# Attention scores by 128 queries of one head, the two heads in the row halves of TensorE's array, for ten of 24 head pairs of a fused attention and gated MLP kernel

## The chip, the cores and the metric

The kernel runs on one core of one Trainium2 chip. The metric is the time of one execution on the device in microseconds (us).

## The reference

Causal attention over 4 batches of 12 heads, 448 positions, head size 64, in single precision; its output, with the heads joined to 768 features, goes through a gated MLP with a spatial product:

```python
scores = scale * np.matmul(q, k.transpose(0, 1, 3, 2))
scores = np.where(np.triu(np.ones((seq, seq), dtype=bool), k=1), -1000000000.0, scores)
attn = np.exp(scores - np.max(scores, axis=-1, keepdims=True))
attn = attn / (np.sum(attn, axis=-1, keepdims=True) + 1e-09)
x = np.matmul(attn, v)                       # heads joined: 4 x 448 x 768
h = np.maximum(x @ w_in, 0.0)                # 1024 features
u, v = h[..., :512], h[..., 512:]
v_n = (v - mean(v)) / np.sqrt(var(v) + 1e-06)
v_s = np.einsum('ts,bsd->btd', w_spatial, v_n) + b_spatial[None, :, None]
out = (u * v_s) @ w_out
```

## The kernel before

The kernel handles the 48 heads as 24 pairs, six a batch (`attend`, one call a pair). A pair's steps: load q and k (`load`), turn them so that the head size lies on the partitions, multiply to scores, add the causal mask and find each row's extreme (VectorE, L757), exponential with its row sum (ScalarE, L769), reciprocal of the sum (L782, L790), scale the weights, turn them, multiply with V (L893), and copy the result into `xT` as a high and a low half-precision part (L911, L916). When a batch's six pairs are there, `ffn` does its matmuls (L1118, 50 us or so of TensorE a batch); chains of them can begin with the pairs that are ready, and otherwise serve as filling between the steps of later pairs.

There are three kinds of pair, set by `TURNED` and `SINGLE`:

- Pairs 0 to 8: q and k are turned by TensorE (`qk_turn`, L578) and kept in single precision. q is laid out in blocks of 128 columns, 64 queries of head 0 in the upper rows and of head 1 in the lower, zeros elsewhere (`q32`, cleared once in `constants`); so one product of the full array (L736) gives the scores of 64 queries of both heads. Seven such products a pair, against 64, 128, ... 448 keys, lie in four PSUM banks (`BANKS`). The weights, in single precision, are scaled by GpSimd, ScalarE or VectorE (`even`, L427, L425, L423), turned by TensorE in 16 blocks (L807) and copied to `et` (L827, L829); the product with V is in single precision, one head in each column half of the array.
- Pairs 9 to 14: the same scores, with widths rounded up to 128 columns, but the weights are split into two half-precision parts (L425, L857) and turned by three DMA transposes (L870); the product with V takes three half-precision terms.
- Pairs 15 to 23: q and k too are split into half-precision parts (two squares and a sum for a scale, L495 and L504; scaling and splitting at L427 and L459), turned by a DMA transpose (L639) and copied across partitions by two local DMAs (L647). The scores are two half-precision products for each 64 queries and head (L746, L747), one head in each column half.

PSUM has four slots `ps` for scores and transposes, one `px` and three `pf` for the feed-forward chains. The order of all work is written out before the run by a planner (`Plan`): it gives each operation a cost in ns for each engine that can do it, spreads the free ones over ScalarE, VectorE and GpSimd, and simulates the engines, taking by rank, which comes from due times. The constants `TUNE`, `SLACK`, `EARLY` and others set the due times and slacks. Each engine and the DMA queue of SyncE then run their instructions in that order.

Of the kernel before, what the change touches and what calls it, by code (L numbers as in the profile page):

```python
# [7 lines left out]
F32 = mybir.dt.float32  # L8
# [240 lines left out]
def kernel(  # L249
# [11 lines left out]
    nc = tc.nc  # L261
# [254 lines left out]
    def constants():  # L516
        nc.vector.memset(ones, 1.0)
        nc.gpsimd.memset(ident, 1.0)
        nc.gpsimd.affine_select(
            out=ident, in_=ident, pattern=[[-1, 128]], compare_op=ALU.is_equal, fill=0.0, base=0, channel_multiplier=1  # L520
        )
        nc.gpsimd.memset(mask, 0.0)
        for h in range(2):
            nc.gpsimd.affine_select(
                out=mask[64 * h:64 * h + 64, 384:448], in_=mask[64 * h:64 * h + 64, 384:448],
                pattern=[[-1, 64]], compare_op=ALU.is_ge, fill=NEG, base=0, channel_multiplier=1,
            )
        nc.gpsimd.memset(mask[:, S:512], NEG)
        for t in phys["e"]:
# [12 lines left out]
        nc.vector.memset(wacc, 0.0)  # L542
        nc.vector.memset(mhalf, -0.5)

    def load(p):
# [4 lines left out]
        for n, src in enumerate((q, k)):  # L550
# [13 lines left out]
                [], [(s["qk"], n)], rank, 448,  # L564
            )

    def qk_turn(p):

        s = st[p]
        rank = 100 * p - 150  # L570
        t = s["qkT"] = Buf("qkT")
        for n in range(2):
            pt = Buf("ps")

            def turn(e, n=n, pt=pt):
                src = at(s["qk"])[:, n].rearrange("p (c h) d -> p c (h d)", h=2)
                for c in range(NCH):
                    nc.tensor.transpose(  # L578
                        out=at(pt)[:, CP * c:CP * c + CP], in_=src[:, c], identity=ident[:CP, :CP]
                    )  # L580

            plan.add(
                {"PE": 470}, turn, [(s["qk"], (n, 0)), (s["qk"], (n, 1)), const_key("ident")],
                [(pt, 0), (t, "room")], rank + n, 200,
            )
            parts = [(slice(0, 64), 0), (slice(64, 128), 64)] if n == 0 else [(slice(0, 128), None)]
            for i, (rows, c0) in enumerate(parts):

                def copy(e, pt=pt, rows=rows, c0=c0):
                    src = at(pt)[rows, :S]  # L590
                    if c0 is None:
                        dst = k32(at(t))
# [9 lines left out]
        s["qkT_keys"] = [(t, (0, 0)), (t, (0, 1)), (t, (1, 0))]  # L602

    def qk_prepare(p):
        if WHOLE[p]:
# [24 lines left out]
        for n in range(2):  # L630
# [4 lines left out]
            )  # L635
        w = s["qkT"] = Buf("qkT")
        s["qkT_keys"] = [(w, 0), (w, 1), (w, 2)]
        dma(
            lambda e: nc.sync.dma_start_transpose(  # L639
                out=at(w)[:, 0:4 * S].rearrange("p (c r) -> p c r", r=CP),  # L640
                in_=at(t).rearrange("p a b c -> p (a b c)"),
            ),
            [(t, "h0"), (t, "l0"), (t, "h1"), (t, "l1")], [(w, 0)], rank + 3, 112, "transpose",
        )
        for n in range(2):
# [53 lines left out]
    AV_TERMS = [(0, 0), (0, 1), (1, 0)]  # L699
    held = {}  # L700

    def attend(p):
        s = st[p]
        b, pi = divmod(p, NP)
# [2 lines left out]
        eb = es = Buf("e")  # L707
        et = Buf("et")

        def pad(e):  # L710

            if held.get(es.slot, True) != turns:
                if turns:
# [4 lines left out]
            held[es.slot] = turns  # L718

        plan.add({"POOL": 100}, pad, [], [(es, "pad")], 100 * p)  # L720
        rank = 100 * p
        for g, units in enumerate(BANKS):
            ps, sm = Buf("ps"), Buf("sm")

            place, at0 = {}, 0
# [128 lines left out]
            for u, (c, (w, part, src)) in enumerate(parts.items()):  # L854
# [8 lines left out]
        if turns:  # L863
# [17 lines left out]
        def av(e):  # L881
            for j in range(4):
                kk = 128 if j < 3 else 64
                n = NU - 2 * j
                for t, (a, w) in enumerate(AV_TERMS[:1] if turns else AV_TERMS):
                    for h in range(2):
                        if turns:
                            lhsT = at(vnat[p])[:kk, 2 * (pi % 3) + h, j, :]
                            rhs = e32(at(et))[:kk, 7 * j:7 * j + n, 64 * h:64 * h + 64]
                        else:  # L890
                            lhsT = at(s["vs"])[:kk, 4 * h + j, 64 * w:64 * w + 64]
                            rhs = e16(at(et))[:kk, ET0[j] + a:ET0[j] + 2 * n:2, 64 * h:64 * h + 64]
# [521 lines left out]
```

## Time and profile before

| | |
|---|---|
| median of 3 runs | 406.49 us (405.89 to 406.72) |
| profiled execution | 406.36 us, span 404.6 us, mean granted TensorE clock 0.981 |
| TensorE busy | 371.9 us (92%) |
| VectorE busy | 280.7 us (69%) |
| ScalarE busy | 259.2 us (64%) |
| GpSimd busy | 198.1 us (49%) |
| bytes moved by DMA | 55.60 MB, mean 137 GB/s |

The span is from the first to the last instruction of the program. Busy shares are of the whole span and mix stages with different limits. PE is TensorE, DVE VectorE, ACT ScalarE, POOL GpSimd, SP the DMA queue's engine; L757 is line 757 of the kernel. Matmuls overlap, so the durations of single records do not add up to the engine's time; the distance from one start to the next does.

### The profile page before, as it was taken

Reading aid. Unit: us, or ns where it says so; the run is one execution under the profiler, and the core shown is the slowest. Engines: PE = TensorE matmul, PEld = TensorE weight load, DVE = VectorE, ACT = ScalarE, POOL = GpSimd, SP = SyncE. Lnnn points to the kernel's source line nnn. Section 1 sums busy time; section 2 is a strip of 40 time slices with the busy share of each in tenths; the row PEclk is TensorE's granted clock in tenths of the full one; section 3 lists DMA queues with packets and bytes.
Section 4 is the critical chain, followed back from the end, with each engine's and each line's share of the span. In section 5 each row is a group of like instructions: output and inputs, shape, how many; then the busy total and the mean of one; then the engine's idle time right before and its main releaser. Section 6 shows DMA issues by size and latency. Waiting matters only on the chain. (4 is left out here: it accounts for less than half of the span.)

```text
span 404.6 us, 7631 instructions
## 1 busy us (share of the span) xinstructions
PE 371.9 (92%) x2438; PEld 231.4 (57%) x2438; DVE 280.7 (69%) x955; ACT 259.2 (64%) x744; POOL 198.1 (49%) x276
## 2 busy tenths in 40 slices
PE   5578869997999999999999999999996999999995
PEld 4455444663556466865545459855452568445595
DVE  4366868889767997977887898676996884031211
ACT  3779867688977566997867957666763655123120
POOL 2310489566887665006289387525892340054120
PEclk9899998999999999999999999999996999999999
DMA  8974882346193349997979978998775546400013
GB/s 176 235 154 145 222 170 101 105 95 148 43 219 87 118 123 172 172 226 174 192 161 206 169 135 191 190 208 197 128 137 105 98 87 120 129 2 0 0 48 109
DMA packets 156298, 55.60 MB, mean 137 GB/s; under 512 B 150177, under 2 KB 152034, under 8 KB 156258
## 3 DMA queue, kind: packets, MB, share of 16 engines
q1 hardware_dynamic: 156258, 55.12, 65.0%
q8 instruction: 19, 0.31, 0.3%
q14 instruction: 21, 0.17, 0.1%
HBM read 26.76 MB, written 5.51 MB: 80 GB/s over the span
## 5 line engine op out<-in xcount | busy, mean ns | idle before, releaser
L736 PE MATMUL ps<-qkT 128*128 128x64 f32 (+6 forms) x210 | 61.7, 422 | 6.8 <-ACT et L827 3.4
L769 ACT ACTIVATE ps<-ps,sm 128x384 f32<-128x384 f32 (+4 forms) x105 | 48.7, 464 | 29.6 <-DVE sm L757 21.6
L1118 PE MATMUL pf<-xT,wi 128*128 128x448 f16 x288 | 62.9, 356 | 0.2 <-ACT u L1265 0.2
L1118 PE MATMUL pf<-wi,xT 128*128 128x512 f16 (+1 forms) x360 | 62.3, 340 | 0.0
L1118 PE MATMUL pf<-wo,g 128*128 128x384 f32 x288 | 59.3, 351 | 0.2 <-DVE u L1291 0.2
L857 DVE SCALAR_TENSOR_TENSOR e<-ps,sm,e 128x256 f16<-128x256 f32 (+4 forms) x105 | 49.4, 504 | 9.4 <-ACT e L425 8.7
L427 POOL TENSOR_SCALAR e<-e,sm 128x64 f32<-128x64 f32 (+6 forms) x51 | 31.1, 626 | 49.4 <-DVE sm L790 33.8
L757 DVE CUSTOM_DVE_ANT_0 ps<-ps,mask 128x384 f32<-128x384 f32 (+6 forms) x105 | 44.1, 443 | 15.5 <-PE ps L736 14.7
L425 ACT ACTIVATE e<-ps,sm 128x384 f16<-128x384 f32 (+4 forms) x105 | 46.2, 507 | 13.3 <-DVE sm L790 9.5
L1118 PEld LDWEIGHTS pf<-wo,g 128*128 128x128 f32 x288 | 49.7, 188 | 4.6 <-issue 2.7
L1118 PE MATMUL pf<-wst,vn 128*128 128x448 f16 (+1 forms) x192 | 42.8, 364 | 4.4 <-ACT u L1265 3.8
L1118 PEld LDWEIGHTS <-xT 128*128 128x128 f16 (+1 forms) x360 | 26.4, 103 | 32.6 <-issue 11.9
L736 PEld LDWEIGHTS ps<-qkT 128*128 128x128 f32 x210 | 33.0, 199 | 16.3 <-ACT et L827 5.1
L1118 PEld LDWEIGHTS <-wi 128*128 128x128 f16 x288 | 26.0, 98 | 27.4 <-issue 7.5
L782 DVE TENSOR_SCALAR sm<-sm 128x2 f32<-128x2 f32 x96 | 24.1, 263 | 20.1 <-ACT e L769 10.4
L769 ACT ACTIVATE e<-ps,sm 128x384 f32<-128x384 f32 (+6 forms) x63 | 29.2, 476 | 11.7 <-DVE sm L757 10.0
L757 DVE CUSTOM_DVE_ANT_0 ps<-ps,mask,sc 128x384 f32<-128x384 f32 (+4 forms) x63 | 30.8, 504 | 4.4 <-PE ps L747 3.7
L427 POOL TENSOR_SCALAR vs<-vnat,vsc 128x512 f16<-128x512 f32 x15 | 10.5, 701 | 45.7 <-PE px L893 41.1
L1118 PEld LDWEIGHTS <-vn 128*128 128x128 f16 (+1 forms) x192 | 18.5, 100 | 23.7 <-issue 9.5
L807 PE MATMUL ps<-ident,e 128*128 128x128 f32 x144 | 22.1, 286 | 8.6 <-POOL e L427 5.2
L1211 POOL TENSOR_TENSOR ln<-ln,mhalf 128x1 f32<-128x1 f32 (+1 forms) x16 | 9.2, 581 | 36.7 <-DVE ln L1203 36.7
L807 PEld LDWEIGHTS ps<-ident,e 128*128 128x128 f32 x144 | 16.7, 145 | 17.2 <-POOL e L427 9.3
(122 smaller groups left out, 699.1 us busy)
## 6 DMA issues: line engine op xcount, KB each, us to landing
wb<-in_moe_w_in_dram SPq DMA_DIRECT2D x12, 512.0 KB, 4.0
vnat<-in_v_dram SPq DMA_DIRECT2D x24, 192.0 KB, 3.7
out_dram<-o SPq DMA_DIRECT2D x12, 384.0 KB, 3.3
qk<-in_q_dram SPq DMA_DIRECT2D x30, 112.0 KB, 3.7
qk<-in_k_dram SPq DMA_DIRECT2D x30, 112.0 KB, 3.7
o<-in_moe_w_out_dram SPq DMA_DIRECT2D x8, 384.0 KB, 3.4
qk<-in_q_dram SPq DMA_DIRECT2D x9, 224.0 KB, 3.8
qk<-in_k_dram SPq DMA_DIRECT2D x9, 224.0 KB, 4.3
```

The costliest lines, as they stand in the source:

```text
L425: nc.scalar.activation(out=dst, in_=src, func=AF.Copy, scale=scale)
L427: nc.gpsimd.tensor_scalar(out=dst, in0=src, scalar1=scale, scalar2=1.0, op0=ALU.mult, op1=ALU.mult)
L736: nc.tensor.matmul(out=at(ps)[:, o0:o0 + n], lhsT=q32(t)[:, c, :], rhs=k32(t)[:, :n], start=True, stop=True)
L757: lambda e, ps=ps, n=n, u=u, sm=sm, o0=o0, m0=m0: nc.vector.tensor_tensor_reduce(out=at(ps)[:, o0:o0 + n], in0=at(ps)[:, o0:o0 + n], in1=m ...
L769: nc.scalar.activation(out=dst, in_=src, func=AF.Exp, scale=-1.0, bias=at(sm)[:, u:u + 1], accum_out=at(sm)[:, 4 + u:5 + u],)
L782: lambda e, n=n, sm=sm, esc=esc: nc.vector.tensor_scalar(out=at(sm)[:, 8:8 + n], in0=at(sm)[:, 4:4 + n], scalar1=1.0 / esc, scalar2=1e-9 / ...
L807: nc.tensor.transpose(out=at(pt)[:, 128 * i:128 * i + 128], in_=e32(at(eb))[:, E0[c] + j, :], identity=ident)
L857: lambda e, part=part, src=src, sm=sm, u=u: nc.vector.scalar_tensor_tensor(out=part(1), in0=src(), scalar=at(sm)[:, 8 + u:9 + u], in1=part(0),
L1118: nc.tensor.matmul(out=o, lhsT=a(), rhs=rhs, start=(n0 + n == 0), stop=(n0 + n == len(mms) - 1), skip_group_check=len(out_ap()) > 1,)
L1211: lambda e, ln=ln, tn=tn: nc.gpsimd.tensor_tensor(out=at(ln)[:tn, 8:9], in0=at(ln)[:tn, 8:9], in1=mhalf[:tn], op=ALU.pow),
```

## The change

Pairs that are both single and turned (`WIDE`) get scores by a new function `wide`: 128 queries of one head per product, with the 64 rows of head 0 in the upper row half of the array and those of head 1 in the lower, each head in PSUM banks of its own; the last 64 queries of both heads share one bank, in its two partition halves. q is kept flat (`flat32`), so that one copy takes the place of two. `mask2`, a causal mask for 128 rows, lies in an unused part of the first `e` buffer. Five groups of scores take five banks; the sums of the groups are in three small buffers; the weights of each group are scaled, turned in 3 or 4 blocks and copied to `et`, which is laid out by head. Turned pairs are now 0 to 9 and single pairs 0 to 11: pairs 10 and 11 are the kind of 9 to 14 before, and pairs 12 to 23 the kind of 15 to 23 before. The two pairs that use the block layout of q clear it first. Six `sm` buffers in place of three, and other constants of the planner.

```diff
+WIDE_PE = 760, 740, 850
-EARLY = 20570
+EARLY = 14463
-TURNED = frozenset(range(9))
-SINGLE = frozenset(range(15))
-SLACK = 345.0, 270.0, 0.0, 100.0, 412.0, 440.0
-TUNE = 23000.0, 5468.0, 44064.0, 3408.0, 785.0, 805.0, 3458.0, 21900.0, 6260.0, 15846.0
+TURNED = frozenset(range(10))
+SINGLE = frozenset(range(12))
+SLACK = 393.0, 184.0, 0, 40.0, 412.0, 440.0
+TUNE = 23000.0, 2734.0, 79315.0, 3238.0, 1066.0, 884.0, 3458.0, 18815.0, 6260.0, 15846.0
...
+    WIDE = [t and w for t, w in zip(TURNS, WHOLE)]
+    mask2 = phys["e"][0][:, 17 * 128:21 * 128]
+    def flat32(t):
+        return t.bitcast(F32)[:, 0:S]
-    store("sm", 3, [128, 16], F32)
+    store("sm", 6, [128, 16], F32)
...
+        nc.gpsimd.memset(mask2[:, 0:384], 0.0)
+        nc.gpsimd.memset(mask2[:, 384:512], 0.0)
+        nc.gpsimd.affine_select(
+            out=mask2[:, 384:512], in_=mask2[:, 384:512], pattern=[[-1, 128]], compare_op=ALU.is_ge, fill=NEG,
...
-        if any(WHOLE):
-            for t in phys["qkT"]:
-                nc.vector.memset(q32(t), 0.0)
...
+        if not WIDE[p]:
+            def clear(e):
+                if not blank.get(at(t).name):
+                    nc.gpsimd.memset(q32(at(t)), 0.0)
+                    blank[at(t).name] = True
+            plan.add({"POOL": 300}, clear, [], [(t, (0, 0)), (t, (0, 1))], rank)
-            parts = [(slice(0, 64), 0), (slice(64, 128), 64)] if n == 0 else [(slice(0, 128), None)]
+            parts = [(slice(0, 64), 0), (slice(64, 128), 64)] if n == 0 and not WIDE[p] else [(slice(0, 128), None)]
...
+    GROUPS = [
+        [(0, 0, 128, 0, 0), (0, 128, 256, 128, 1)],
+        [(1, 0, 128, 0, 3), (1, 128, 256, 128, 4)],
+        [(0, 256, 384, 0, 6)],
+        [(1, 256, 384, 0, 9)],
+        [(None, 384, S, 0, 12)],
+    ]
+    def wide(p, eb, et):
+        s, rank = st[p], 100 * p
+        banks = [Buf("ps") for _ in GROUPS]
+        def product(h, q0, n, bank, o0, r0, rn):
+            t = at(s["qkT"])
+            rows = slice(64 * h, 64 * h + 64)
+            nc.tensor.matmul(
+                out=at(bank)[r0:r0 + rn, o0:o0 + n], lhsT=flat32(t)[rows, q0:q0 + rn], rhs=k32(t)[rows, :n],
+                start=True, stop=True, skip_group_check=True,
+            )
+        def both(g):
+            for i in range(len(GROUPS[g])):
+                for h in range(2):
+                    _, q0, n, o0, _ = GROUPS[g + h][i]
+                    product(h, q0, n, banks[g + h], o0, 0, 128)
+        def last():
+            for h in range(2):
+                product(h, 384, S, banks[4], 0, 64 * h, 64)
+        sums = [Buf("sm") for _ in range(3)]
+        whose = [(sums[g // 2], 2 * (g % 2) if g < 2 else g % 2) for g in range(5)]
+        for n, fn in enumerate((lambda e: both(0), lambda e: both(2), lambda e: last())):
+            parts = [(banks[g], u) for g in (2 * n, 2 * n + 1) if g < 5 for u in range(len(GROUPS[g]))]
+            plan.add({"PE": WIDE_PE[n]}, fn, s["qkT_keys"], parts + [(eb, "room")], rank)
...
+            for i in range(2 if g < 2 else 1):
+                def copy(e, pt=pt, i=i, g=g):
+                    by_head = at(et).rearrange("p (h r) -> p h r", h=2)
...
+                plan.add({"ACT": c_act(n, "P"), "DVE": c_dve(n)}, copy, [(pt, 0)], [(et, (g, i))], rank)
...
-        for g, units in enumerate(BANKS):
+        if WIDE[p]:
+            wide(p, eb, et)
+        for g, units in enumerate(() if WIDE[p] else BANKS):
...
+                            if WIDE[p]:
+                                rhs = at(et)[:kk, 1408 * h + 448 * j:1408 * h + 320 * j + S]
```

Left out are the lines of `wide` that mask, exponentiate, sum, scale and turn each group, which follow those of `attend` with the group's widths.

## Rows read from the trace of the kernel before

**Rows 1.** Page, the span in 40 equal slices: tenths busy of TensorE.
```profile
PE   5578869997999999999999999999996999999995
```

**Rows 2.** Busy by stage: stretch, each engine's us and instructions, clock, DMA share, GB/s.
```profile
0.00:60.00 60.00, 42.67 (x232) 28.01 (x232) 36.62 (x152) 43.53 (x126) 19.82 (x48) 0.97 0.86 185
...
100.00:300.00 200.00, 196.46 (x1400) 121.29 (x1400) 165.79 (x584) 147.78 (x433) 119.73 (x158) 1.00 0.81 161
300.00:315.00 15.00, 11.24 (x57) 4.73 (x56) 11.30 (x25) 6.12 (x21) 6.02 (x8) 0.77 0.64 120
315.00:350.00 35.00, 35.00 (x271) 23.63 (x268) 20.96 (x66) 19.31 (x54) 8.47 (x12) 1.00 0.59 125
350.00:404.60 54.60, 50.09 (x286) 32.51 (x284) 10.99 (x25) 11.41 (x21) 14.72 (x18) 0.98 0.09 29
```

**Rows 3.** Chain that ended last, from 340 us: start, us, what.
```profile
347.83 1.55 PE px L893 x24
...
364.71 35.55 PE pf L1118 x195
```

**Rows 4.** Timeline, 301 to 309, VectorE, GpSimd, TensorE: start, us, group, [idle before, releaser].
```profile
301.87 4.69 DVE L438 SCALAR_TENSOR_TENSOR vs<-vnat,vsc,vs 128x512 f16<-128x512 f32 x1
...
303.08 2.26 POOL L459 TENSOR_TENSOR qks<-qk,qks 112x512 f16<-112x512 f32 x2
...
308.15 1.28 PE L1118 MATMUL pf<-wst,vn 128*128 128x448 f16 x3 [3.76 <-ACT u L1265]
```

**Rows 5.** Timeline of TensorE, 23 to 28 and 65 to 68.
```profile
23.99 0.28 PE L504 MATMUL px<-vsc,ones 128*128 128x1 f32 x2
25.02 2.10 PE L893 MATMUL px<-et,vnat 128*64 128x448 f32 x16 [0.75 <-DVE vsc L466]
27.05 0.41 PE L578 MATMUL ps<-ident,qk 112*128 112x112 f32 x2
...
65.37 2.64 PE L736 MATMUL ps<-qkT 128*128 128x192 f32 x10
67.85 0.38 PE L1118 MATMUL pf<-wi,xT 128*128 128x512 f16 x1
```

**Rows 6.** Timeline of TensorE, 327 to 332, a pair in half precision.
```profile
327.32 1.62 PE L893 MATMUL px<-et,vs 128*64 128x448 f16 x24
328.87 0.28 PE L746 MATMUL ps<-qkT 128*64 128x192 f16 x2
...
330.46 0.28 PE L746 MATMUL ps<-qkT 128*64 128x256 f16 x2
330.57 0.28 PE L747 MATMUL ps<-qkT 128*64 128x256 f16 x2
330.78 0.80 PE L1118 MATMUL pf<-wo,g 128*128 128x384 f32 x3
331.50 0.38 PE L746 MATMUL ps<-qkT 128*64 128x448 f16 x2
...
332.01 1.31 PE L1118 MATMUL pf<-wo,g 128*128 128x384 f32 x6
```

**Rows 7.** Timeline of TensorE, 126 to 128: transposes of q or k, then of weights.
```profile
126.18 0.55 PE L578 MATMUL ps<-ident,qk 112*128 112x112 f32 x4
126.66 0.63 PE L807 MATMUL ps<-ident,e 128*128 128x128 f32 x4
127.13 0.73 PE L1118 MATMUL pf<-wst,vn 128*128 128x448 f16 x3
```

**Rows 8.** Page, costliest groups: count | busy us, mean ns | idle before, releaser.
```profile
L736 PE MATMUL ps<-qkT 128*128 128x64 f32 (+6 forms) x210 | 61.7, 422 | 6.8 <-ACT et L827 3.4
```

**Rows 9.** Groups by line, GpSimd and ScalarE.
```profile
L459 POOL TENSOR_TENSOR qks<-qk,qks 112x512 f16<-112x512 f32 x18 | 20.5, 1158 | 0.0
...
L597 ACT ACTIVATE qkT<-ps 64x448 f32<-64x448 f32 (+1 forms) x39 | 20.9, 541 | 3.8 <-PE ps L578 3.0 <-DVE qkT L599 0.5
```

**Rows 10.** Busy by stage, 160 to 300, columns as in rows 2.
```profile
160.00:300.00 140.00, 138.05 (x1042) 85.73 (x1039) 115.86 (x424) 106.44 (x318) 76.77 (x100) 1.00 0.92 177
```

More of the change, by code (lines that the diff above doesn't have):

```diff
@@ L565, in load @@
             )
+    blank = {}
     def qk_turn(p):
@@ L585, in qk_turn, with copy @@
             )
[L586 removed]
+            parts = [(slice(0, 64), 0), (slice(64, 128), 64)] if n == 0 and not WIDE[p] else [(slice(0, 128), None)]
             for i, (rows, c0) in enumerate(parts):
[L589 removed]
+                def copy(e, pt=pt, rows=rows, c0=c0, n=n):
                     src = at(pt)[rows, :S]
                     if c0 is None:
[L592 removed]
+                        dst = k32(at(t)) if n else flat32(at(t))
+                        if not n:
+                            blank[at(t).name] = False
                     else:
@@ L700, with even, turn @@
     held = {}
+    GROUPS = [
[5 more added lines that the diff above has]
+    ]
+    HR = 1408
+    def wide(p, eb, et):
[7 more added lines that the diff above has]
+                start=True, stop=True, skip_group_check=True,
+            )
+        def both(g):
[11 more added lines that the diff above has]
+            plan.add({"PE": WIDE_PE[n]}, fn, s["qkT_keys"], parts + [(eb, "room")], rank)
+        for g, (ps, group) in enumerate(zip(banks, GROUPS)):
+            sm, u0 = whose[g]
+            for u, (h, q0, n, o0, _) in enumerate(group):
+                plan.add(
+                    {"DVE": c_dve(n) + 8},
+                    lambda e, ps=ps, n=n, u=u0 + u, sm=sm, o0=o0, h=h: nc.vector.tensor_tensor_reduce(
+                        out=at(ps)[:, o0:o0 + n], in0=at(ps)[:, o0:o0 + n],
+                        in1=mask[:, 0:n] if h is None else mask2[:, 512 - n:512],
+                        scale=-0.125, scalar=3.0e38, op0=ALU.add, op1=ALU.min, accum_out=at(sm)[:, u:u + 1],
+                    ),
+                    [const_key("mask")], [(ps, u), (sm, f"m{u0 + u}")], rank,
+                )
+            for u, (_, _, n, o0, c) in enumerate(group):
+                plan.add(
+                    {"ACT": c_act(n, "P", 2)},
+                    lambda e, ps=ps, n=n, u=u0 + u, sm=sm, o0=o0, c=c: nc.scalar.activation(
+                        out=at(eb)[:, 128 * c:128 * c + n], in_=at(ps)[:, o0:o0 + n], func=AF.Exp, scale=-1.0,
+                        bias=at(sm)[:, u:u + 1], accum_out=at(sm)[:, 4 + u:5 + u],
+                    ),
+                    [(sm, f"m{u0 + v}") for v in range(len(group))], [(ps, u), (sm, f"s{u0 + u}"), (eb, c)], rank,
+                )
+        for n, sm in enumerate(sums):
+            m = (4, 2, 1)[n]
+            plan.add(
+                {"DVE": 250},
+                lambda e, m=m, sm=sm: nc.vector.tensor_scalar(
+                    out=at(sm)[:, 8:8 + m], in0=at(sm)[:, 4:4 + m], scalar1=1.0, scalar2=1e-9, op0=ALU.mult, op1=ALU.add,
+                ),
+                [(sm, f"s{u}") for u in range(m)], [(sm, "d")], rank,
+            )
+            plan.add(
+                {"DVE": 150},
+                lambda e, m=m, sm=sm: nc.vector.reciprocal(out=at(sm)[:, 8:8 + m], in_=at(sm)[:, 8:8 + m]),
+                [], [(sm, "d")], rank,
+            )
+        for g, group in enumerate(GROUPS):
+            sm, u0 = whose[g]
+            for u, (_, _, n, _, c) in enumerate(group, u0):
+                def even(e, c=c, u=u, sm=sm, n=n):
+                    w = at(eb)[:, 128 * c:128 * c + n]
+                    scaled_copy(e, w, w, at(sm)[:, 8 + u:9 + u])
+                plan.add(
+                    {"POOL": 260 + 1.25 * n, "ACT": c_act(n, "S", 1), "DVE": c_fast(n, 1)}, even, [(sm, "d")],
+                    [(eb, c)], rank,
+                )
+            pt = Buf("ps")
+            c0, cn = group[0][4], 4 if g == 4 else 3
+            def turn(e, pt=pt, c0=c0, cn=cn):
+                for i in range(cn):
+                    nc.tensor.transpose(
+                        out=at(pt)[:, 128 * i:128 * i + 128], in_=e32(at(eb))[:, c0 + i, :], identity=ident
+                    )
+            plan.add(
+                {"PE": cn * 116}, turn, [(eb, x[4]) for x in group] + [(eb, "pad"), const_key("ident")], [(pt, 0)],
+                rank, 200,
+            )
+            for i in range(2 if g < 2 else 1):
+                def copy(e, pt=pt, i=i, g=g):
+                    by_head = at(et).rearrange("p (h r) -> p h r", h=2)
+                    blocks = at(pt)[:, 0:384].rearrange("p (j r) -> p j r", r=128)
+                    if g < 2:
+                        src, dst = at(pt)[:, 0:256], by_head[:, g, 0:256]
+                        if i:
+                            src, dst = at(pt)[:, 256:384], by_head[:, g, 448:576]
+                    elif g < 4:
+                        src = blocks
+                        dst = by_head[:, g - 2, 256:256 + 960].rearrange("p (j r) -> p j r", r=320)[:, :, 0:128]
+                    else:
+                        src = at(pt).rearrange("p (j h r) -> p j h r", j=4, h=2)
+                        dst = by_head[:, :, 128:HR].rearrange("p h (j r) -> p j h r", r=320)[:, :, :, 256:320]
+                    if e == "ACT":
+                        nc.scalar.activation(out=dst, in_=src, func=AF.Copy)
+                    else:
+                        nc.vector.tensor_copy(out=dst, in_=src)
+                n = (256, 128)[i] if g < 2 else 128 * cn
+                plan.add({"ACT": c_act(n, "P"), "DVE": c_dve(n)}, copy, [(pt, 0)], [(et, (g, i))], rank)
@@ L862, in attend @@
                 )
-        if turns:
+        if WIDE[p]:
+            et_keys = [(et, (g, i)) for g in range(5) for i in ((0, 1) if g < 2 else (0,))]
+        elif turns:
             et_keys = [(et, (g, i)) for g in range(4) for i in ((0, 1) if g == 1 else (0,))]
```

22 lines of the change are left out of this document (15 added, 7 removed).

## The prediction

> **What bounds the kernel now.** I read the slices first, then busy time by stage, then the chain that ended last, and only then single stretches of the timeline. The slices [rows 1] show TensorE busy in 9 tenths or more of nearly every slice after the seventh, and in 5 to 8 before it. The stages say the same in microseconds [rows 2]: 42.67 of the first 60 us, then, at the full clock, 196.46 of the 200 us from 100 to 300, where VectorE has 165.79, ScalarE 147.78 and GpSimd 119.73. So behind 60 us another microsecond of matmul is a microsecond of time, unless it fits a gap; before 60 us TensorE waits for others. At the end lie more than 50 us of feed-forward matmuls of the last batch, with VectorE at 10.99 [rows 2]; the last 35.55 us of the chain are one run of them [rows 3]. The change does not touch that run: it can only start sooner.
>
> One hole in the middle is worth knowing. At 301.87 a 512-column VectorE instruction shows 4.69 us while GpSimd works through its run of instructions for the next pair without a pause; TensorE then sits idle for 3.76 us before 308.15 [rows 4]. In the stretch around it the granted clock is 0.77 [rows 2], that is 15 x 0.23 = 3.45 us of clock lost. One such stall costs 7.2 us.
>
> **The change, part by part.** Three kinds of pair exist. Call turned pairs, with single-precision scores and attention weights turned by TensorE, A; pairs with single-precision scores and weights turned by DMA, B; pairs in split half precision, C. Before: A 0 to 8, B 9 to 14, C 15 to 23. After: new A 0 to 9, B 10 and 11, C 12 to 23.
>
> *Scores of A.* Before, seven products per pair with 64 queries of each head, widths 64 to 448, 1,792 columns in all. Five of them, 1,344 columns, run from 65.37 to 67.85 [rows 5]: 1.85 ns a column, 3.31 us a pair. After, the widths are 128, 256, 384 and 448 for each head, 1,216 columns, if the two heads run at once. No row shows two products in the two row halves. The nearest is the product with V of an A pair, two heads in the two column halves: 1,024 columns for each head from 25.02 to 27.05 [rows 5], 1.98 ns a column for both together, against 1.85 for one. So both heads there cost hardly more than one. For row halves that gives 1,216 x 1.85 to 1.98 = 2.25 to 2.41 us. The bound from the other side is that they do not overlap: 2,432 x 1.85 = 4.5 us. I take 2.33, by the row that shows two heads at once.
>
> A change of the array's shape costs time: half-precision score passes of 256 columns start 0.11 us apart (330.46, 330.57), but the full-array product behind the last starts 0.21 us after it (330.78) [rows 6]: 0.10 us each. Three groups of scores in half rows, each left and entered, make six, 0.6 us; where groups follow each other there are fewer. I take 0.43. A wide pair is 2.76 us and saves 0.55; bounds +1.0 saved (no change of shape) and, without overlap, 4.5 + 0.6 - 3.31 = 1.8 lost.
>
> A rule that speaks against this: the Trainium skill, "TensorE: Matmul & The Clock Gate", section "LDWEIGHTS (loading the stationary operand)", says that a weight load takes its columns at 1.2 GHz however few its rows are. Two heads then load 2 x 128 columns for each pass, 0.21 us as an estimate from that page, where the 128-column pass streams for half of that; it would add 0.2 us to each wide pair and make the sum below 400 in place of 399. No run here shows it.
>
> *Pair 9, from B to A.* Its scores save the 0.55 too. It gains 16 transposes of weights, at 126.66 to 127.13 for four [rows 7], 1.88 us, and pays 2.03 us in place of 1.55 [rows 5, 6] for the product with V, 0.48 more. Together +1.8 on TensorE. It drops three DMA transposes.
>
> *Pairs 12 to 14, from B to C.* Gone are the single-precision scores, 3.31, and eight transposes of q and k, 0.48 for four [rows 7], 0.96. In their place come half-precision scores: 448 columns take 0.51 us (331.50 to 332.01, a change of shape included) [rows 6], 1.14 ns a column, and 1,984 columns 2.26 us; and one small sum by two matmuls, 0.28 [rows 5]. Net 1.73 saved a pair, 5.2 for three. On GpSimd each such pair brings two subtractions of 1.16 us [rows 9], 7 us for three, in a stage where it is 60% busy [rows 2]. By the code each brings a transpose of 459 kB and two local copies of 115 kB to the DMA queue. From 160 to 300 the engines are 0.92 busy at 177 GB/s [rows 10], so 192 GB/s is full, and 688 kB are 3.6 us, 10.8 for three. DMA idles 11 us in that stretch and 20 more between 300 and 350 [rows 2]. It hides there, with 31 - 7 = 24 us left when the time shrinks by 7; without that cover it is 10.8 us.
>
> *Vector work of A.* One copy of q in place of two saves 0.54 us a pair [rows 9]; 192 more columns of mask, exponential and scaling and two more copies out of PSUM cost about as much. Nothing, then, in engines that TensorE hides after 60 us. At the start, the copy may save up to 0.54 us once; I take 0.5. The mask built by GpSimd is wanted only by the first scores; two clears of a buffer go from VectorE, and clears for pairs 10 and 11 come to GpSimd a pair ahead of use: nothing.
>
> *The plan anew.* Due times and slacks move everything. The trace cannot price that; I assume that the new order keeps TensorE as full as the old one and has one stall like the one at 301.87.
>
> *Sum*, against the profiled execution's 406.36 us (span 404.6, 1.8 around it). Behind 60 us: four wide pairs (5 to 8) -2.2; pair 9 +1.8; pairs 12 to 14 -5.2; together -5.6. Before 60 us: five wide pairs save 2.75 us on a TensorE that is 71% busy; between 0 and 2.75 I take 1.2; the copy 0.5. In all -7.3: 399.1, and the median of the runs is 0.1 higher, so 399.
>
> **The rivals.** (B) *Banks.* A wide pair takes five score banks and five transpose banks out of four slots, and its first product asks for two at once; with q and k twelve in place of ten. Score products already wait 6.8 us in all before they start, most of it for a ScalarE copy that frees a bank [rows 8], 0.45 a pair. Doubled for ten pairs it takes back 4.5 us: 403.5. Against it: feed-forward products fill such waits after 60 us. The Trainium skill, "TensorEngine Tiling (Array Packing)", section "PSUM Bottleneck", says that tiling speeds up TensorE and not the evacuation; the waits in these rows bear it out in part, and 403.5 is what it would give.
>
> (C) *Stalls of VectorE by GpSimd*, on the other side. Three more C pairs mean three more of the GpSimd runs seen in [rows 4]; each can hold VectorE until TensorE falls idle and the clock falls with it, at 7.2 us each. One more leaves 406, two more give 413; from two on it decides. Against it: one of the nine C pairs shows such a stall now.
>
> (D) *The row halves do not run at once.* Then pairs 5 to 9 lose 1.8 in place of winning 0.55, 12 us, and the early pairs some 4 us: 415. It decides from 3.7 us a wide pair on, at which the savings are gone. That the change does not do what it says is this case.
>
> (E) *The hole closes*: the new order has no stall of that size: 399 - 7 = 392.
>
> **How the numbers follow.** The forecast has 0.58, with a range of its own from 393 to 403; B 0.18, C 0.11, D 0.06, E 0.07. Two tenths of a per cent is about what a measurement of this kernel can tell from no change: 405.7 to 407.3. Faster: forecast, E and 0.13 of B, 0.78; same: 0.05 of B and 0.01 of C; slower: 0.10 of C and D, 0.16. The range 389 to 408 leaves out D, most of C and the low end of E.
>
> **What would show each step.** Right: score records of 64 rows whose two heads start a few ns apart, a wide pair in 2.5 to 3 us when its groups are added; ten pairs with DVE and ACT score groups of 128 to 448 columns and 12 with half-precision scores; TensorE still above 95% from 100 to 300; the product with V of the last pair some 7 us sooner than at 347.83 [rows 3], and the run behind it as long as before. Wrong: heads that follow each other by a whole pass (D); score products that wait for ScalarE copies for over 10 us (B); a VectorE instruction of several microseconds with TensorE idle behind it (C), or none (E); DMA at full share from 160 to the last pair, with TensorE waiting for a transpose.

## The result and the profile after

The changed kernel takes 410.16 us (median of 20 runs, 406.16 to 413.86) against 405.97 (404.12 to 408.9) in as many runs of the kernel before: a ratio of 1.0091 with a 95% interval of [1.0067, 1.0115]. Here and below, the ratio leaves out runs in a slower state (here the three slowest of the changed kernel) and so can differ from the quotient of the medians. The changed kernel is slower; forecast were 399 us and a range that ends at 408. Its profiled execution, 406.16 us with a span of 404.4, is the fastest of the twenty; a second profile, of an execution of 413.86 us (span 412.1, experiment 1), is read beside it.

The page: slices of the span (tenths of TensorE, of its clock, and of DMA), and two of its costliest groups:

```profile
PE   5869698887999987999789998999998999999995
PEclk9968999999999999999998999999999999999999
DMA  7996664508194493997989999899855856200013
...
L468 POOL TENSOR_TENSOR qks<-qk,qks 112x512 f16<-112x512 f32 x24 | 28.7, 1211 | 0.0
...
L752 PE MATMUL ps<-qkT 64*64 64x448 f32 (+3 forms) x160 | 29.9, 462 | 4.2 <-ACT e L787 4.2
```

The first row answers to [rows 1]: there are fewer nines between the tenth slice and the thirtieth. Busy time by stage, columns as in [rows 2]:

```profile
0.00:60.00 60.00, 46.32 (x258) 25.79 (x259) 37.52 (x153) 45.23 (x142) 20.76 (x50) 0.91 0.82 189
60.00:100.00 40.00, 32.74 (x209) 17.02 (x208) 34.60 (x109) 31.11 (x97) 28.17 (x34) 1.00 0.45 116
100.00:300.00 200.00, 188.12 (x1396) 113.64 (x1396) 168.07 (x556) 138.65 (x421) 139.22 (x182) 0.98 0.84 165
300.00:315.00 15.00, 13.42 (x108) 6.99 (x103) 13.52 (x42) 7.72 (x24) 9.40 (x12) 1.00 0.58 110
...
350.00:404.40 54.40, 49.88 (x285) 32.34 (x283) 10.18 (x24) 11.52 (x21) 14.55 (x18) 0.98 0.09 30
160.00:300.00 140.00, 133.48 (x1051) 82.84 (x1051) 115.53 (x405) 96.58 (x296) 85.64 (x109) 0.98 0.97 182
```

From 100 to 300 us TensorE is busy 188.12 us, where it was 196.46 [rows 2], at 0.98 of the clock in place of 1.00. The matmul work that was taken away has left holes; it has not shortened the stage. VectorE stands as before (168.07 against 165.79), GpSimd has risen from 119.73 to 139.22, and from 160 to 300 DMA is 0.97 busy where it was 0.92 [rows 10]. From 300 to 315, where before TensorE stood idle behind the stall of [rows 4], it is busy for 13.42 of 15 us at the full clock, in place of 11.24 at 0.77 [rows 2].

The chain that ended last, as in [rows 3]:

```profile
304.49 3.67 DVE sm L942 x3
...
345.64 1.55 PE px L1057 x24
347.19 16.57 PE pf L1282 x99
364.47 35.58 PE pf L1282 x195
```

The product with V of the last pair starts 2.2 us sooner than at 347.83, and what stands behind it is 2.0 us longer (404.4 - 345.64 = 58.8 against 404.6 - 347.83 = 56.8). In the second profile the product starts at 353.34, 5.5 us later than before, with the same 58.8 us behind it.

*What the changed parts cost.* Timeline of TensorE around wide pairs:

```profile
66.73 0.93 PE L752 MATMUL ps<-qkT 64*128 64x128 f32 x8
67.59 0.87 PE L824 MATMUL ps<-ident,e 128*128 128x128 f32 x6
...
70.42 0.92 PE L752 MATMUL ps<-qkT 64*128 64x384 f32 x4
71.27 0.55 PE L824 MATMUL ps<-ident,e 128*128 128x128 f32 x3
...
85.61 1.82 PE L752 MATMUL ps<-qkT 64*64 64x448 f32 x12
87.36 0.38 PE L513 MATMUL px<-wacc,ones 128*128 128x1 f32 x2
```

The first group of scores, 384 columns for each head, takes 0.86 us from start to next start, the second, 384 too, 0.85; the twelve at 85.61 are a last group and a first one, 1.75, so 0.89 for the last. That is 2.60 us a pair. One head after the other would take 2 x 384 x 1.85 ns = 1.42 us for a group by the price of [rows 5]: the row halves do run at once. The first group holds the passes of 128 columns, the second none, and they take the same; so the 0.2 us that the prediction estimated from the weight-load time in the Trainium skill ("TensorE: Matmul & The Clock Gate", "LDWEIGHTS (loading the stationary operand)") does not show here.

An account of TensorE, worked out from the distances between the starts of its records (the stream is the time in which columns run through the array, with what the lower clock adds taken out; the rest of each span lies ahead of the first matmul and behind the last):

| us | before | after | after, second profile |
|---|---|---|---|
| stream, at full clock | 322.3 | 310.6 | 309.8 |
| gaps up to 0.25 us (changes of shape) | 36.2 | 40.1 | 39.6 |
| gaps over 0.25 us | 31.8 | 38.7 | 44.5 |
| of these from 60 to 200 us | 8.5 | 17.6 | 16.5 |
| lost to the lower clock | 5.7 | 6.8 | 9.6 |

Stream and small gaps fall by 7.8 us in the first profile, and long gaps and clock give back 8.0; in the second 9.1 against 16.6. The saving is there, and TensorE waits it away.

### The profile page after: what moved, and what is told of

The parts are those of the page before. It is cut to its first block, busy times and chain, and to the rows that moved or that the text cites. A ratio compares the mean times of both kernels' runs of the same rounds, so it can differ in the third digit from the quotient of the medians.

```text
span 404.4 us, 7801 instructions
## 1 busy us (share of the span) xinstructions
PE 365.0 (90%) x2490; PEld 219.5 (54%) x2490; DVE 284.0 (70%) x942; ACT 252.1 (62%) x754; POOL 220.3 (54%) x304
## 3 DMA queue, kind: packets, MB, share of 16 engines
q1 hardware_dynamic: 157922, 56.14, 66.4%
## 4 chain that ended last, share of the span: by engine, by line
PE 40%; DVE 23%; ACT 18%; DMA 7%; issue 4%; POOL 4%; SPq 3%; ACTq 0%; POOLq 0%; DVEq 0%
PE pf L1282 28%; ACT ps L929 4%; PE px L1057 4%; ACT junk L504 4%; DVE ps L917 4%; ACT e L434 3%; DVE e L1017 3%; DMA wb<-in_moe_w_in_dram 3%; DMA et<-e 3%; PE ps L824 2%; ACT e L787 2%; DVE ps L777 2%; PE ps L896 2%; DVE sc L488 2%; SPq L566 1%
## 5 line engine op out<-in xcount | busy, mean ns | idle before, releaser
L1282 PE MATMUL pf<-wo,g 128*128 128x384 f32 x288 | 58.8, 350 | 2.0 <-ACT o L1491 2.0
L436 POOL TENSOR_SCALAR e<-e,sm 128x128 f32<-128x128 f32 (+3 forms) x57 | 33.1, 594 | 41.4 <-DVE sm L804 20.0
L434 ACT ACTIVATE e<-ps,sm 128x384 f16<-128x384 f32 (+4 forms) x98 | 40.5, 514 | 3.9 <-DVE sm L950 3.8
L787 ACT ACTIVATE e<-ps,sm 128x256 f32<-128x256 f32 (+3 forms) x70 | 34.4, 504 | 10.2 <-DVE sm L777 9.7
L917 DVE CUSTOM_DVE_ANT_0 ps<-ps,mask,sc 128x384 f32<-128x384 f32 (+4 forms) x84 | 38.7, 505 | 1.5 <-PE ps L907 1.0
L752 PE MATMUL ps<-qkT 64*64 64x448 f32 (+3 forms) x160 | 29.9, 462 | 4.2 <-ACT e L787 4.2
L777 DVE CUSTOM_DVE_ANT_0 ps<-ps,e 128x256 f32<-128x256 f32 (+2 forms) x60 | 24.5, 439 | 9.9 <-issue 5.7
L468 POOL TENSOR_TENSOR qks<-qk,qks 112x512 f16<-112x512 f32 x24 | 28.7, 1211 | 0.0
L849 ACT ACTIVATE et<-ps 128x256 f32<-128x256 f32 (+3 forms) x60 | 23.6, 436 | 8.0 <-PE ps L824 7.8
L942 DVE TENSOR_SCALAR sm<-sm 128x2 f32<-128x2 f32 (+1 forms) x56 | 20.9, 384 | 10.2 <-ACT ps L929 9.6
L1057 PE MATMUL px<-et,vs 128*64 128x448 f16 (+3 forms) x336 | 23.8, 284 | 4.2 <-DMA et<-e 4.2
```

What stands on the lines that cost most here:

```text
L434: nc.scalar.activation(out=dst, in_=src, func=AF.Copy, scale=scale)
L436: nc.gpsimd.tensor_scalar(out=dst, in0=src, scalar1=scale, scalar2=1.0, op0=ALU.mult, op1=ALU.mult)
L468: lambda e: HANDLE[e].tensor_tensor(out=dst_l(), in0=src(), in1=dst_h(), op=ALU.subtract),
L752: nc.tensor.matmul(out=at(bank)[r0:r0 + rn, o0:o0 + n], lhsT=flat32(t)[rows, q0:q0 + rn], rhs=k32(t)[rows, :n], start=True, stop=True, ski ...
L777: lambda e, ps=ps, n=n, u=u0 + u, sm=sm, o0=o0, h=h: nc.vector.tensor_tensor_reduce(out=at(ps)[:, o0:o0 + n], in0=at(ps)[:, o0:o0 + n], in ...
L787: lambda e, ps=ps, n=n, u=u0 + u, sm=sm, o0=o0, c=c: nc.scalar.activation(out=at(eb)[:, 128 * c:128 * c + n], in_=at(ps)[:, o0:o0 + n], fu ...
```

## Experiments

**Which part costs the time (1 to 9).** (1) The changed kernel again.

> The changed kernel once more, for its time beside the kernel before and a second profile. Theory DMA (three more pairs in split half precision fill the DMA engines between the tenth pair and the last, so the TensorE time that the new scores save turns into waits for transposes): about 410 us again, 1% slower than before, the profile with a DMA share of 0.95 or more from 160 to 300 us and products with V that wait for a DMA transpose. Theory plan (the new due times and slacks order the work worse): the same time, with the holes of TensorE before 160 us. Theory banks (five banks of wide scores in four slots): the same time, with score products waiting over 10 us for ScalarE.

412.86 us, ratio 1.0167 [1.0131, 1.0202]. The loss repeats, and is larger; no run shows why. This interval and the first one, [1.0067, 1.0115], do not overlap, so the changed kernel's own time is known to some 3 us, and its edits below are to be read against both ratios. DMA is not 0.95 busy from 160 to 300 us in this profile, as the DMA theory wanted, but 0.90, less than before:

```profile
160.00:300.00 140.00, 130.09 (x989) 82.69 (x989) 116.86 (x390) 92.50 (x287) 80.78 (x104) 0.96 0.90 176
```

(2) The wide scores with the mixture of pairs and the constants of before; (3) the mixture without wide scores, and (4) with them, both under the old constants. The edits are against the changed kernel:

```diff
(2) -TURNED = frozenset(range(10))
    -SINGLE = frozenset(range(12))
    +TURNED = frozenset(range(9))
    +SINGLE = frozenset(range(15))
    EARLY, SLACK, TUNE as before
(3) -    WIDE = [t and w for t, w in zip(TURNS, WHOLE)]
    +    WIDE = [False for t, w in zip(TURNS, WHOLE)]
    EARLY, SLACK, TUNE as before
(4) EARLY, SLACK, TUNE as before
```

> Wide scores alone: pairs 0 to 8 turned and wide, 0 to 14 single, the planner's constants as before the change. Theory DMA: no DMA is added, so nine pairs at 0.7 us saved show, 400 to 403 us. Theory plan: also faster than before, 400 to 403. Theory banks: no gain or a loss, 405 to 411.

> The other mixture of pairs alone: scores by blocks as before for all single pairs, turned pairs 0 to 9, single pairs 0 to 11, the planner's constants as before the change. Theory DMA: slower than before in spite of 3.6 us less TensorE work, 408 to 413 us, DMA share 0.95 or more from 160 to 300. Theory plan: faster than before by the work saved, 402 to 405. Theory banks: the same 402 to 405.

> The changed kernel with the planner's constants (due times, slacks, head start) of before. Theory plan: 397 to 402 us, the forecast. Theory DMA: 406 to 412, as the changed kernel. Theory banks: 406 to 412.

(2) 405.07 us, 0.9972 [0.9941, 1.0002]; (3) 419.35, 1.0358 [1.0318, 1.0398]; (4) 421.46, 1.0394 [1.0352, 1.0436]. Wide scores alone, in nine pairs that each save over half a microsecond of TensorE, win about a microsecond that is not clear of noise: the interval reaches from 2.4 us faster to no change. Under the old constants the mixture costs 13 us without wide scores, (3) against the kernel before, and 16 with them, (4) against (2). So the theory that the new constants pack worse falls: (4) differs from the changed kernel in them alone, and they win back 11 us. A stage of (3), columns as in [rows 2]:

```profile
100.00:200.00 100.00, 88.27 (x522) 57.55 (x517) 82.19 (x247) 66.07 (x195) 70.22 (x93) 0.95 0.60 131
```

No engine is busy for the whole stage, and TensorE has its lower clock in part of it.

(5, 6) The two halves of the mixture, each added to (2); (7, 8) each taken out of the changed kernel, new constants kept; (9) the changed kernel with one old constant.

```diff
(5) TURNED = frozenset(range(10)), SINGLE = frozenset(range(15)), old constants
(6) TURNED = frozenset(range(9)), SINGLE = frozenset(range(12)), old constants
(7) -SINGLE = frozenset(range(12))
    +SINGLE = frozenset(range(15))
(8) -TURNED = frozenset(range(10))
    +TURNED = frozenset(range(9))
(9) -EARLY = 14463
    +EARLY = 20570
```

> wide_alone with pair 9 turned by TensorE as well (turned 0 to 9, single 0 to 14, old constants). If the tenth turned pair is what the mixture costs there: 412 to 418 us. If the split pairs are: 403 to 406.

> wide_alone with pairs 12 to 14 split (turned 0 to 8, single 0 to 11, old constants). If the three added split pairs are what the mixture costs there: 412 to 418 us. If the tenth turned pair is: 403 to 406. If it is the order, which fits neither: both of these above 408.

> The changed kernel with pairs 12 to 14 left single (turned 0 to 9, single 0 to 14, new constants): wide scores and pair 9 turned, but no added split pair. Theory DMA queue: three qk transposes and six local copies less, 398 to 404 us, in spite of 5 us more TensorE work. Theory pair 9 (turning it loads VectorE and GpSimd between 100 and 200 us and delays all that follows): 408 to 414. Theory TensorE: 5 us slower than the changed kernel, 415.

> The changed kernel with pair 9 turned by DMA as before (turned 0 to 8, single 0 to 11, new constants): wide scores and the added split pairs, but no tenth turned pair. Theory DMA queue: three transposes of weights more, 410 to 418 us. Theory pair 9: 400 to 405.

> The changed kernel with the head start of before (20570 in place of 14463), all else as changed. If the hole between 60 and 100 us hangs on it: 403 to 407 us, under 5 us of long TensorE gaps there. If not: 410 to 413.

(5) 410.29 us, 1.0078 [1.0046, 1.0109]: pair 9 by TensorE costs 5 us over (2). Its last pair comes 5 us sooner than in (2) (product with V at 343.2 against 348.4), but 66.4 us of work stand behind it in place of 52.6: the feed-forward products had been pushed back. (6) 412.42, 1.0155 [1.0117, 1.0193]: three more C pairs, forecast to save 5.2 us of matmul, cost 7. Both are above 408, the sign that was named for the order as the cause. (7) 408.74, 1.0067 [1.0044, 1.009], not told apart from the changed kernel (the intervals overlap): wide scores and a turned pair 9 lose under the new constants without the three added C pairs too. In its profile 64 us stand behind the last product with V, in place of 57 before. (8) 420.06, 1.0328 [1.0297, 1.0358]: under the new constants the turned pair is needed, 10 us, where under the old ones it costs 5. (9) 418.87, 1.03 [1.0273, 1.0328]; its long gaps from 60 to 100 us are 9.1 us, as in the changed kernel (8.4; before 3.6), so they do not hang on `EARLY`. An edit has no price of its own here: it has one in an order.

**Does TensorE set the pace (10, 11)?** 72 matmuls left out of the chains for `u` of batches 0 to 2, some 13.5 us of TensorE:

```diff
-    def chain(ps, out_ap, mms, cost, keys, due):
+    def chain(ps, out_ap, mms, cost, keys, due, drop=False):
...
+                    if drop and n == 1:
+                        continue
...
-                c_pe(S), [], r0 + FSTEP * (4 + f),
+                c_pe(S), [], r0 + FSTEP * (4 + f), b < 3,
```

> The kernel before, order unchanged, without one of the three matmul terms in the chains of the first 512 features of batches 0 to 2: 72 matmuls of 448 columns less, 13.5 us of TensorE, between 60 us and the last batch; the output lacks those terms. The premise of the forecast (behind 60 us a microsecond of matmul is a microsecond of time): 392 to 394 us. Theory order (the written order and the steps of the pairs set the pace, and feed-forward matmuls only fill the holes that they leave): 400 to 406.

> The changed kernel without the same 72 matmuls. The premise of the forecast: 13.5 us less, 397 us. Theory order: 406 to 411, TensorE idle longer by most of the 13.5 us.

In the kernel before 404.95 us, 0.9969 [0.9949, 0.9989]; in the changed one 412.01, 1.0164 [1.013, 1.0199]. 13.5 us of matmul are worth 1.3 us in the one and nothing that shows in the other. The stages of the first:

```profile
100.00:200.00 100.00, 94.80 (x589) 59.37 (x587) 82.95 (x291) 77.63 (x224) 51.34 (x69) 1.00 0.70 147
200.00:300.00 100.00, 94.12 (x760) 56.99 (x757) 84.41 (x298) 70.91 (x213) 69.34 (x90) 1.00 0.93 175
```

TensorE falls to 188.92 of 200 us, and the time all but stays: the picture of the changed kernel, without any of the change.

**What sets it, then (12 to 17)?** From the product with V of pair 10 to that of pair 23 it is 171.5 us before and 170.1 in (10), 172.8 and 175.6 in the two profiles after and 175.7 in (11): in the same order, 13.5 us less of matmul hardly bring the pairs closer together. Another order does move it, from 164.6 in (5) to 177.8 in (3). Two of the steps of those pairs are now taken away, the order unchanged. (12, 13) No local copies in the DMA queue; the second half-precision product reads other rows in their place. (14, 15) Six GpSimd instructions of each C pair on 8 of 64 features; VectorE clears their buffers once at the start, 0.9 us. (16, 17) Both.

```diff
(12, 13)
-                lambda e, n=n: nc.sync.dma_start(
-                    out=qk16(w)[64 - 64 * n:128 - 64 * n, 4:6, :], in_=qk16(w)[64 * n:64 * n + 64, 2:4, :]
-                ),
+                lambda e: None,
...
-                        nc.tensor.matmul(out=o, lhsT=w, rhs=qkT[:, 4 + x, :n], start=False, stop=True)
+                        nc.tensor.matmul(out=o, lhsT=w, rhs=qkT[:, 2 + x, :n], start=False, stop=True)
(14, 15)
+        for t in phys["qks"]:
+            nc.vector.memset(t, 0.0)
...
-                "qk"[n], lambda n=n: at(t)[:, n, :, 0:64], lambda n=n: at(t)[:, n, :, 64:128], lambda n=n: at(s["qk"])[:, n],
+                "qk"[n], lambda n=n: at(t)[:, n, :, 0:8], lambda n=n: at(t)[:, n, :, 64:72], lambda n=n: at(s["qk"])[:, n, :, 0:8],
```

> The kernel before without the two local copies of its nine split pairs, scores lacking their cross terms, order unchanged. Theory DMA queue: if the queue sets the pace in the kernel before too, 396 to 401 us; if TensorE does there and the queue only after the change, 404 to 406. Theory VectorE and GpSimd: 404 to 406.

> The changed kernel without the two local DMA copies of each of the 12 split pairs (2.75 MB, 1.1 us of issue a pair); the second score product of each block reads the part of k that is already there, so the scores lack their cross terms; the planned order is the same. Theory DMA queue (from the tenth pair on the queue and the engines behind it set the pace of a pair, 13 us): 12 pairs at about 1.2 us, 396 to 402 us. Theory VectorE and GpSimd (their load between 100 and 200 us and the steps of a split pair set the pace): 408 to 412 us, no change. Theory TensorE: no change.

> The kernel before, order unchanged, with GpSimd's six instructions that scale and split q and k of a pair working on 8 of 64 features (the rest of q and k stays zero in the scores): about 4 us of GpSimd less for each of nine split pairs. Theory GpSimd (its runs hold up VectorE, and TensorE waits behind it): 400 to 403 us, without the 4.69 us instruction near 300. Theory TensorE or DMA: 405 to 406.

> The changed kernel with the same six instructions of its 12 split pairs on 8 of 64 features. Theory GpSimd: the gain comes back, 396 to 402 us, with VectorE's excess over its usual durations cut by half. Theory DMA: 406 to 409, TensorE waiting for transposes as before. Theory TensorE: 410.

> The kernel before without the local copies and with the six GpSimd instructions of each split pair on 8 of 64 features. If its pace then is TensorE's, at some 10 us more of TensorE work than the changed kernel: 397 to 399 us, not below before_short_gpsimd. If its pace is that of DMA and the vector engines still: 392 to 396.

> The changed kernel without the local copies and with the six GpSimd instructions of each split pair on 8 of 64 features (scores lack their cross terms and most features). Theory two limits (DMA and GpSimd with VectorE each hold a split pair to about the same pace, so that taking one away leaves the other): 394 to 399 us, the time from the product with V of pair 10 to that of pair 23 down from 173 to 165 us or less. Theory order (the written order itself has the holes): 402 to 406.

| | in the kernel before | in the changed kernel |
|---|---|---|
| no edit | 405.97 | 410.16, 1.0091 [1.0067, 1.0115] |
| no local copies | 405.59, 0.9983 [0.9961, 1.0004] | 407.99, 1.0062 [1.003, 1.0094] |
| GpSimd shortened | 398.24, 0.9807 [0.9785, 0.9829] | 405.35, 0.9964 [0.9934, 0.9993] |
| both | 397.31, 0.9783 [0.9759, 0.9808] | 398.19, 0.9805 [0.9777, 0.9834] |

Before, GpSimd's instructions are worth 8 us and the copies nothing. Where the 8 us lie is seen from the start of each pair's product with V, in us, read from the traces:

| | pair 10 | pair 19 | pair 20 | pair 23 |
|---|---|---|---|---|
| kernel before | 176.3 | 292.6 | 314.9 | 347.8 |
| (10) less matmul | 176.6 | 292.3 | 314.0 | 346.6 |
| (12) no local copies | 175.0 | 290.4 | 311.7 | 344.5 |
| (14) GpSimd shortened | 176.4 | 291.5 | 307.3 | 340.1 |
| (16) both | 176.3 | 290.5 | 305.8 | 338.6 |
| changed kernel | 172.7 | 295.4 | 307.3 | 345.6 |
| (17) changed, both | 171.0 | 288.0 | 299.9 | 337.1 |

In (14) pair 19 comes 1.1 us sooner, pair 20 7.6 us. So nearly all of the 8 us is one place, the hole of [rows 4]: the VectorE instruction that takes 4.69 us there takes 0.76, and TensorE, busy for 11.24 of the 15 us from 300 to 315 at 0.77 of its clock [rows 2], is busy throughout at the full clock:

```profile
299.43 0.76 DVE L438 SCALAR_TENSOR_TENSOR vs<-vnat,vsc,vs 128x512 f16<-128x512 f32 x1
...
300.00:315.00 15.00, 15.00 (x112) 7.70 (x111) 12.27 (x43) 11.01 (x33) 4.94 (x11) 1.00 0.83 154
```

Up to pair 19 none of the four edits of the kernel before moves the pairs by more than some 2 us, so what paces them there is not shown.

In the changed kernel, against its two ratios, GpSimd's work is worth 5 to 8 us, the copies alone 1 to 4 (not told apart from nothing by the first ratio), and both 12 to 15. Once GpSimd is shortened, the copies are worth 7 us (405.35 to 398.19). Taken together they are worth more than one by one: two limits that stand side by side. In (17) the gain on the first profile grows from pair 10, 1.7 us, to pair 23, 8.5 us. Busy time from 200 to 300 us in the kernel before, in (14) and in (16):

```profile
200.00:300.00 100.00, 98.69 (x783) 58.75 (x782) 83.04 (x294) 70.37 (x210) 68.39 (x89) 1.00 0.91 171
200.00:300.00 100.00, 99.19 (x788) 59.32 (x787) 81.81 (x297) 71.16 (x215) 48.08 (x91) 1.00 0.93 176
200.00:300.00 100.00, 100.00 (x796) 59.48 (x794) 82.72 (x303) 72.41 (x219) 49.98 (x96) 1.00 0.87 162
```

In the changed kernel, in (15), and, with the stage ahead of it, in (17):

```profile
200.00:300.00 100.00, 95.84 (x796) 58.03 (x793) 82.68 (x289) 68.90 (x211) 67.63 (x86) 0.98 0.95 179
200.00:300.00 100.00, 95.30 (x788) 58.38 (x788) 75.32 (x285) 68.96 (x211) 41.77 (x85) 0.98 0.94 180
100.00:200.00 100.00, 94.50 (x662) 57.96 (x661) 83.25 (x276) 72.28 (x215) 61.42 (x99) 1.00 0.71 152
200.00:300.00 100.00, 98.69 (x791) 58.45 (x789) 81.24 (x313) 71.75 (x225) 48.17 (x94) 1.00 0.87 165
```

In the kernel before, the stage is full with every edit. In the changed one it keeps its holes with GpSimd shortened and fills only when the copies are gone as well. The DMA share does not tell the cases apart (0.93 with a full TensorE in (14), 0.94 with holes in (15)); leaving the copies out does. In (16) TensorE is full, and 397.31 us lies in the range that was given for a pace set by TensorE; whether it sets the pace once the rest is out of the way is open, as no run takes matmuls out of (16). Even in (17) the change gains nothing (398.19 against 397.31): from 100 to 200 us holes are left.

(18) The scaling and rounding of q and k taken from GpSimd and left to ScalarE and VectorE, planned anew, in (2):

```diff
-            {"ACT": c_act(n, "S", 1), "POOL": c_pool(n, 1), "DVE": c_fast(n, 1)},
+            {"ACT": c_act(n, "S", 1), "DVE": c_fast(n, 1)} if what in "qk" else {"ACT": c_act(n, "S", 1), "POOL": c_pool(n, 1), "DVE": c_fast(n, 1)},
...
-            {"ACT": c_act(n), "POOL": c_pool(n), "DVE": c_fast(n)},
+            {"ACT": c_act(n), "DVE": c_fast(n)} if what in "qk" else {"ACT": c_act(n), "POOL": c_pool(n), "DVE": c_fast(n)},
```

> Wide scores with the old mixture and the old constants (wide_alone), and the scaling and rounding of q and k of split pairs kept off GpSimd, to ScalarE or VectorE; the order is planned with that. Theory GpSimd: 398 to 403 us against 405 of wide_alone. Theory order: 405 to 410, the new order as good or bad as any other.

408.52 us, 1.005 [1.0031, 1.0069]: 3.5 us worse than (2). Moving that work does not do what leaving it out does. Of the kernels that compute everything none beats the one before beyond its interval; (2) is nearest.

## Why the prediction was wrong, step by step

**The step that failed** is "behind 60 us another microsecond of matmul is a microsecond of time", and with it "I assume that the new order keeps TensorE as full as the old one"; the words behind the first, "unless it fits a gap", were given no price. Everything in the sum behind 60 us was put through it at one to one, 5.6 us; (10) prices it at 1.3 us in 13.5. The 196.46 of 200 us in [rows 2] were rightly read, and are no proof of a bound: the feed-forward products fill whatever time the pairs take, so TensorE is full as long as there is enough filling, and takes no less time when there is less. What sets the end is when the last pair is through, and the work that stands behind it. In the changed kernel the pairs are held by their steps through GpSimd and DMA: 12 to 15 us go with both. That the change is not only without gain but slower comes with the mixture, whose halves cost 5 and 7 us in (5) and (6); how much of that is the order alone is not shown, since (7) loses without the added C pairs.

**Terms that were right.** A wide pair: 2.76 us forecast, 2.60 by rows, 2.67 over all ten with the small gaps. All of the change's matmul: 7.8 us less on TensorE in the first profile, where the forecast's terms, wide scores in ten pairs (-5.5), pair 9's transposes and product with V (+2.36) and three C pairs (-5.2), make -8.3. One count was off: the scores at 65.37 [rows 5] are pair 4's, so five wide pairs and not four lie behind 60 us, some 0.3 us in the sum. D is dead: records of the two heads start a few ns apart, 7 at the median.

**B and E.** B is not settled. Score products of wide pairs wait 4.2 us for ScalarE, 0.42 a pair and not the doubled 0.9, but transposes that want one of the same four slots wait behind those exponentials too: 10.8 us in all, where before it was 1.9, and about half of it behind 60 us. The waits of TensorE in the kernel before, then in the changed one (us in total, times, longest):

```profile
PE ps L736 <- ACT e L769: 1.9, 2, 1.6
...
PE ps L601 <- ACT e L787: 5.0, 8, 1.4
PE ps L752 <- ACT e L787: 4.2, 4, 2.1
...
PE ps L824 <- ACT e L787: 1.6, 1, 1.6
```

In (2), with wide scores in nine pairs, 3.3 us of such waits all lie ahead of 60 us, and it gains hardly anything; no run gives wide scores more banks. E came in part: no hole of that size is left at 300 us, but the time did not follow, as long gaps rose from 31.8 to 38.7 us elsewhere.

**The DMA term** was costed at nothing under 24 us of cover. Of the 11 us that DMA idled from 160 to 300 about 4 are left in the first profile (0.97 busy) and 14 in the second (0.90), which is the slower one, so the idle share is no price. The copies, 0 to 1 us before, are worth 1 to 4 us now and 7 once GpSimd is shortened. The cover was counted over a stage in which, by the code, a pair's transfer has to land before its own scores, not at some time in the stage.

**The GpSimd term**, 7 us "in a stage where it is 60% busy", was costed at nothing, and it was too small: the traces have six GpSimd instructions for q and k in each C pair, not two, and their busy time rises from 44.4 to 61.4 us, by 17, of which the subtractions are 8 (L468, 28.7 against 20.5 [rows 9]). Rival C named the mechanism and had 0.11, but it came in another form: not one or two stalls of 7.2 us but many short ones. The changed kernel's VectorE and GpSimd, timeline:

```profile
212.60 0.14 DVE L942 TENSOR_SCALAR sm<-sm 128x2 f32<-128x2 f32 x1
...
216.58 1.85 DVE L488 TENSOR_SCALAR sc<-sc 128x2 int32<-128x2 int32 x1
...
304.42 3.75 DVE L942 TENSOR_SCALAR sm<-sm 128x2 f32<-128x2 f32 x3
...
216.66 1.16 POOL L1406 TENSOR_TENSOR vn<-hv,vn 128x512 f16<-128x512 f32 x1
217.79 0.62 POOL L436 TENSOR_SCALAR vn<-hv 128x512 f16<-128x512 f32 x1
...
304.63 2.27 POOL L1406 TENSOR_TENSOR vn<-hv,vn 128x512 f16<-128x512 f32 x2
306.85 1.16 POOL L468 TENSOR_TENSOR qks<-qk,qks 112x512 f16<-112x512 f32 x1
308.00 0.72 POOL L436 TENSOR_SCALAR vs<-vnat,vsc 128x512 f16<-128x512 f32 x1
```

Two columns take 0.14 us at 212.60. At 216.58 they take 1.85, to 218.43, when GpSimd has finished its run (217.79 + 0.62 = 218.41); at 304.42 the first of three such instructions alone takes 3.62 of the 3.75, to 308.04, when GpSimd's last operation on two tensors has ended (306.85 + 1.16 = 308.01); they are in the chain that ended last. Added over all VectorE instructions that exceed the shortest times of their shape by more than 0.4 us, this is some 23 us before and 33 after (35 in the second profile), 22 in (2), 34 in (6), and 19 in (15): it comes with the three C pairs and goes with GpSimd's work. It is not the whole loss: in (7) it is 19 us, and (7) is not told apart from the changed kernel. In (14) the gain is mostly one such hold; how much of (15) is this holding and how much GpSimd's own time in each pair's chain of steps, no run separates.

**What stays open.** The long gaps from 60 to 200 us, 17.6 us after against 8.5 before. The causes inferred for them are many and short; the largest in the list of TensorE's waits for that stretch are:

```profile
PE px L1057 <- DMA et<-e: 2.4, 1, 2.4
PE ps L601 <- ACT e L787: 2.2, 3, 0.9
PE ps L824 <- DVE e L1017: 1.9, 1, 1.9
PE ps L824 <- POOL e L436: 1.9, 1, 1.9
```

Which of the new constants places them, beyond that it is not `EARLY`, was not tried. Nor is it known what paces the pairs up to pair 19 in the kernel before, and why the changed kernel spreads from 406 to 414 us.

## What to carry to other kernels

An engine at 98% in a stage is not thereby its bound, where work that can go anywhere fills its gaps: before counting a microsecond of it as one of time, leave some of that filling out and see whether the end moves. In a chain of pairs, follow one kind of work (here the product with V) from pair to pair, in the same order: 171.5 us that become 170.1 with 13.5 us less of matmul say that TensorE is not the limit, and the pair at which an edit gains says whether it relieved a pace or closed one hole. And a change that trades matmul for transfers and for GpSimd is costed on the chain of each item that gets them, not against the idle share of a stage.

## What the runs showed of the hardware

A two-column VectorE instruction was held for 1.85 us while GpSimd went through two instructions, and another for 3.62 us over three of GpSimd's. One of 512 columns took 4.69 us beside a run of GpSimd instructions and 0.76 us when these were short. The Trainium skill, "SBUF — State Buffer", "Who interferes with whom", says that a VectorE instruction in a mode that uses two ports contends with GpSimd, and that whoever issues first has the shared pair of ports for the whole instruction while the other blocks. The ends that fall together agree, and the rows show that the wait can run on past one GpSimd instruction into the next ones; in which mode these instructions were, no run here shows.

Single-precision products of 64 rows in the two row halves ran at once at about the price of one: 384 columns for each of two heads in 0.85 us, the change of shape included, where 384 alone cost 0.71 by [rows 5].
